# Reading a product in PSUM: two activations from the bank, scores copied by the maximum, a bank for helper products

## The chip, the cores and the metric

The kernel runs on one core of one Trainium2 chip. The metric is the device time of one execution in microseconds, median of several runs.

## The reference

Four batches of attention (8 heads, 576 tokens, 64 columns a head), and on its output, 2304 tokens by 512 columns, two expert layers one after the other. In the attention only scores within tau of their row's maximum count:

```python
scores = scale * np.matmul(q, k.transpose(0, 1, 3, 2))
thresh = np.max(scores, axis=-1, keepdims=True) - tau
scores = np.where(scores >= thresh, scores, -1000000000.0)
attn = np.exp(scores - np.max(scores, axis=-1, keepdims=True))
attn = attn / (np.sum(attn, axis=-1, keepdims=True) + 1e-09)
x = np.matmul(attn, v)
...
h = x @ w_in                                   # first layer, 512 -> 2048
P = a[0] + a[1] * h + a[2] * h**2 + a[3] * h**3
Q = 1.0 + np.abs(b[0]) * np.abs(h) + np.abs(b[1]) * h**2
y = (P / (Q + 1e-06)) @ w_out                  # 2048 -> 512
...
h = y @ w2_in                                  # second layer
g = np.where(h >= 1, h, np.where(h <= -1, 0.0, (h + 1) ** 2 / 4))
out = g @ w2_out
```

## The kernel before

Every number that enters a product is scaled and split into two float16 parts, high and low, and each product is three products of parts, added up in PSUM.

The work after the attention is cut into 192 steps: four batches, two layers, three blocks of 192 tokens, eight chunks of 256 hidden columns. A step is first_product (24 matmuls of 128x192 into one PSUM bank, tag "ph"; then the layer's function, rational or quadratic, on 128x384 elements; then split into gg on ACT and POOL) and, three steps later (LAG), second_product (24 matmuls into the accumulator, two banks, tag "acc").

rational begins with an ACT copy of the bank to h in SBUF, scaled (L517); all else reads h. ACT takes |h|, a logarithm and an exponential for the quotient, and one linear term; VectorE and POOL do the polynomials. For batch 0 the denominator's polynomial is done on POOL (L522, L523), for the others on VectorE (L520); s times h is POOL's for all (L527). quadratic too begins with an ACT copy (L581), then a Relu on ACT and two instructions on VectorE (L583, L584).

Attention of batch 0 runs first, beside the conversion of the first layer's weights. Attention of batch b + 1 is put beside the steps of batch b. It has 17 units per batch: five prepare inputs (units 0, 1, 2, 5 and 9), twelve do three rows each. A row is 128 queries of one head (att_rows): scores into two PSUM banks (tag "s", two tiles, for batch 0 a third in the accumulator's place), their maximum on VectorE (L406), a small instruction for the threshold (L407), the exponential on ACT (L368) and the mask on VectorE (L369), both from PSUM; then e is split into hl on ACT and POOL, transposed by DMA into eT, multiplied with v (tag "pv"; for batch 0 "ph"), divided by its sum (normalize), transposed by TensorE and stored as xT, from which the batch's first layer reads.

Small products that spread a maximum over the partitions (everywhere), the transposes in normalize and those of the output all take the bank with tag "pv". PSUM is full: one bank "pv", one "ph", two "acc", four "s".

A scheduler puts each engine's instructions in one order from priorities: a step's is its number, its second product's 1.5 later, a unit of attention's its due step less 1.5. The due steps are spread evenly over the window in ATTENTION, steps 6 to 46 for batch 1, 52 to 95 for batch 2, 100 to 143 for batch 3; the first layers of these batches begin at steps 48, 96 and 144. Each engine then works strictly in its order and waits where an input is late or a buffer is taken.

## Time and profile before

| | us |
|---|---|
| median of 3 runs | 1382.62 (1377.87 to 1388.38) |
| profiled execution | 1375.72 |
| its span, first to last instruction | 1373.6 |

Engines are PE (TensorE matmul), PEld (TensorE weight load), DVE (VectorE), ACT (ScalarE), POOL (GpSimd); SP issues the DMAs. Busy time is that in which an engine has an instruction at work; a VectorE or POOL instruction that is held up by the other counts as busy. A wait is named by the instruction whose end released it. L517 is line 517 of the kernel.

### The profile page before, as it was taken

To read this page: it belongs to the slowest core of one execution; us is meant where nothing else is said; L and a number is where in the kernel's file an instruction comes from. 1 tells how busy PE (TensorE), PEld (TensorE's weight loads), DVE (VectorE), ACT (ScalarE), POOL (GpSimd) and SP (SyncE) were. 2 spreads that over 40 slices of the span, in tenths; PEclk is the share of its full clock that TensorE was granted. 3 is DMA by queue.
4 is the path that set the end of the run, shared out by engine and by line. 5 is a ranking of instruction groups with operands and counts; after the bars stand their busy time and mean duration, and the time that the engine had idled before them with its cause. 6 is when DMAs were issued, how large, how long until landed. Compare 5 with 4: busy or idle time off the path is not lost. (4 is left out here: it accounts for less than half of the span.)

```text
span 1373.6 us, 31370 instructions
## 1 busy us (share of the span) xinstructions
PE 1075.8 (78%) x12498; PEld 979.7 (71%) x12498; DVE 1079.4 (79%) x2209; ACT 882.5 (64%) x1563; POOL 686.1 (50%) x716
## 2 busy tenths in 40 slices
PE   1545445566766398999978999987889898999998
PEld 1233234565655388898878889986788888988998
DVE  6787776899999967758999886599998665788422
ACT  4766555676756566667776666677766565777543
POOL 2755454887856454443655534435554344444221
PEclk9765556798887599999999999999999999999999
DMA  7879776325368745294238643923295449104200
GB/s 212 217 170 250 173 202 203 108 83 139 101 203 229 221 108 105 56 285 118 55 56 242 139 99 67 301 61 72 53 252 115 74 69 271 52 1 171 77 13 24
DMA packets 260274, 187.11 MB, mean 136 GB/s; under 512 B 220960, under 2 KB 233248, under 8 KB 251936
## 3 DMA queue, kind: packets, MB, share of 16 engines
q1 hardware_dynamic: 260128, 185.12, 52.0%
q8 instruction: 98, 1.61, 0.5%
q14 instruction: 48, 0.39, 0.1%
HBM read 106.96 MB, written 21.50 MB: 94 GB/s over the span
## 5 line engine op out<-in xcount | busy, mean ns | idle before, releaser
L651 PE MATMUL acc<-gg,wc 128*128 128x192 f16 x4608 | 447.8, 253 | 37.9 <-ACT gg L189 22.6
L651 PEld LDWEIGHTS <-wc 128*128 128x128 f16 x4608 | 401.4, 101 | 36.7 <-issue 33.3
L637 PEld LDWEIGHTS <-wc 128*128 128x128 f16 x4608 | 396.0, 100 | 38.4 <-issue 34.4
L190 POOL TENSOR_TENSOR gg<-t,gg 128x384 f16<-128x384 f32 x192 | 193.5, 1008 | 248.2 <-ACT gg L189 231.3
L637 PE MATMUL ph<-xT,wc 128*128 128x192 f16 x2304 | 225.2, 256 | 16.0 <-ACT t L517 14.4
L637 PE MATMUL ph<-yT,wc 128*128 128x192 f16 x2304 | 212.8, 247 | 10.6 <-ACT t L581 10.4
L189 ACT CAST gg<-t 128x384 f16<-128x384 f32 x192 | 97.5, 508 | 141.5 <-DVE t L531 64.2
L379 POOL TENSOR_TENSOR hl<-e,hl 128x512 f16<-128x512 f32 x144 | 181.7, 1261 | 0.0
L527 POOL TENSOR_TENSOR t<-t 128x384 f32<-128x384 f32 x96 | 117.1, 1221 | 120.1 <-ACT t L526 113.0
L377 ACT CAST hl<-e 128x576 f16<-128x576 f32 x144 | 96.0, 669 | 92.2 <-DMA eT<-hl 75.6
L368 ACT ACTIVATE e<-s,nt,con 128x576 f32<-128x576 f32 x144 | 117.9, 827 | 56.7 <-DVE nt L407 43.6
L378 POOL TENSOR_TENSOR hl<-e,hl 128x64 f16<-128x64 f32 x144 | 59.9, 416 | 183.5 <-ACT hl L377 159.8
L583 DVE SCALAR_TENSOR_TENSOR t<-t,c 128x384 f32<-128x384 f32 x96 | 68.3, 712 | 100.4 <-ACT t L582 98.7
L394 PE MATMUL pv<-v,eT 128*128 128x65 f16 (+1 forms) x2240 | 99.6, 208 | 45.5 <-DMA eT<-hl 16.8
L394 PEld LDWEIGHTS <-eT 128*128 128x128 f16 (+1 forms) x2240 | 93.4, 110 | 58.4 <-issue 38.4
L369 DVE SCALAR_TENSOR_TENSOR e<-s,nt,e 128x576 f32<-128x576 f32 x144 | 115.7, 807 | 23.8 <-ACT e L368 23.5
L357 PE MATMUL s<-qkT 128*128 128x512 f16 (+3 forms) x320 | 91.4, 327 | 50.1 <-DVE e L369 30.1
L406 DVE TENSOR_REDUCE mx<-s 128x1 f32<-128x576 f32 x144 | 106.3, 746 | 3.9 <-PE s L358 3.6
L528 DVE SCALAR_TENSOR_TENSOR t<-t,ka 128x384 f32<-128x384 f32 x96 | 87.7, 915 | 15.9 <-POOL t L527 15.9
L524 ACT ACTIVATE t<-t,lc 128x384 f32<-128x384 f32 x96 | 67.5, 703 | 38.2 <-DVE t L520 28.0
L530 DVE SCALAR_TENSOR_TENSOR t<-t,qc 128x384 f32<-128x384 f32 x96 | 78.6, 818 | 6.6 <-ACT t L525 6.6
L358 PE MATMUL s<-kT,qkT 128*128 128x512 f16 (+2 forms) x320 | 74.2, 325 | 9.9 <-DMA kT<-qkT 9.9
(170 smaller groups left out, 1708.8 us busy)
## 6 DMA issues: line engine op xcount, KB each, us to landing
wc<-scratch SPq DMA_DIRECT2D x56, 1024.0 KB, 6.1
rw<-in_moe_w_in_dram SPq DMA_DIRECT2D x16, 1024.0 KB, 5.7
rw<-in_moe_w_out_dram SPq DMA_DIRECT2D x16, 1024.0 KB, 5.6
scratch<-wc SPq DMA_DIRECT2D x8, 1024.0 KB, 4.6
scratch<-wh SPq DMA_DIRECT2D x16, 512.0 KB, 3.3
kT<-qkT SPq DMA_DIRECT2D x32, 144.0 KB, 2.5
rqk<-in_q_dram SPq DMA_DIRECT2D x16, 256.0 KB, 3.1
rqk<-in_k_dram SPq DMA_DIRECT2D x16, 256.0 KB, 3.0
```

What stands on the lines that cost most here:

```text
L189: A.copy(hi, src)
L190: G.tensor_tensor(lo, src, hi, op=ALU.subtract)
L357: T.matmul(s[rows, at : at + w], qkT[:, c, cols], k1[:, k0 : k0 + w], start=True, stop=False)
L368: A.activation(e, s, AF.Exp, bias=nb, scale=con[:, 0:1])
L369: V.scalar_tensor_tensor(e, s, th, e, op0=ALU.is_ge, op1=ALU.mult)
L377: A.copy(hi, e)
L379: G.tensor_tensor(lo_w, e[:, whole], hi[:, whole], op=ALU.subtract)
L394: T.matmul(pv[rows, 0:w], eT[:, c, cols], vv[:, h * NT + x if x < NT else H * NT + h, at : at + w], start=(n == 0), stop=(n == len(blocks) ...
L406: V.tensor_reduce(mx, s[:, 0:S], axis=AX.X, op=ALU.max)
L527: G.tensor_tensor(s, s, h, op=ALU.mult)
L637: last = T.matmul(ph[:, f, :], w[:, wx, kt, f * P : (f + 1) * P], rhs, start=(n == 0), stop=(n == 3 * KT - 1))
L651: T.matmul(dst, w[:, wx, f, d * P : (d + 1) * P], gg[:, gx, f, :], start=(i == 0 and f == 0 and n == 0 and d % 2 == 0), stop=(i == NCH - 1 ...
```

## The change

The bank of the first product is read more often and for longer: ACT's absolute value and linear term, and two VectorE instructions, take it from PSUM, with the scale moved into the constants (three small products per batch in moe1_consts, one per block in moe2_consts); the copy to h is gone in both functions. The denominator's polynomial and s times the product are VectorE's in all batches. There are two "ph" banks. In att_rows the maximum is found by an instruction that multiplies by 1, takes the larger of that and -3e38, writes the result to SBUF and accumulates the maximum; exponential and mask read that copy. One score tile is left, for batch 0 the accumulator's place is the second. Helper products, the transposes and the output's take a bank "aux"; "pv" is the weighted sum's alone. For batch 0 the weighted sum has both "ph" banks. Buffers: five shared temporaries in place of seven (a step of rational takes one in place of two) and three more of half the size ("poly"); two each of e and of the copy in place of three of e; one of xs in place of two. The windows of ATTENTION are 14 to 50, 60 to 100 and 108 to 147.

```diff
--- before.py
+++ after.py
@@ -26,10 +26,10 @@
 LAG = 3
 
 
-N_TEMP, N_WT, N_WH, N_GG, N_ROW = 7, 3, 2, 4, 3
-
-
-ATTENTION = {1: (6, 46), 2: (52, 95), 3: (100, 143)}
+N_TEMP, N_POLY, N_WT, N_WH, N_GG, N_ROW, N_SC = 5, 3, 3, 2, 4, 3, 2
+
+
+ATTENTION = {1: (14, 50), 2: (60, 100), 3: (108, 147)}
 WEIGHTS = (0, 20)
 
 
@@ -162,7 +162,7 @@
 
         r = small(n, name, keep)
         if place is None:
-            place = ps_1.tile([P, 512], F32, name="pm" + name, tag="pv")
+            place = ps_1.tile([P, 512], F32, name="pm" + name, tag="aux")
         pm = place[:, 0 : n * P].rearrange("p (n q) -> p n q", n=n)
         for i in range(n):
             T.matmul(pm[:, i], src[:, i : i + 1].to_broadcast([P, P]), ident, start=True, stop=True)
...
@@ -360,11 +360,10 @@
 
     def softmax(b, s, ab, con, nb, th, name):
 
-        s = s[:, 0:S]
         if b == 0:
             e = mp.tile([P, 2 * W], F32, name="e" + name, tag="tp", bufs=N_TEMP)[:, 0:S]
         else:
-            e = ap.tile([P, S], F32, name="e" + name, tag="e", bufs=N_ROW)
+            e = ap.tile([P, S], F32, name="e" + name, tag="e", bufs=N_SC)
         A.activation(e, s, AF.Exp, bias=nb, scale=con[:, 0:1])
         V.scalar_tensor_tensor(e, s, th, e, op0=ALU.is_ge, op1=ALU.mult)
         hl = ap.tile([P, 2 * S], F16, name="hl" + name, tag="hl", bufs=N_ROW)
@@ -399,15 +398,16 @@
         name = f"{b}_{pr}_{g}"
         rows = ROWS[3 * g : 3 * g + 3]
         for r, (t, ab) in enumerate(rows):
-            third = b == 0 and r == 2
-            s = ps_2.tile([P, 1024], F32, name=f"s{name}_{r}", tag="acc" if third else "s", bufs=1 if third else 2)
-            scores(s, t, ab, qkT, kT2)
+            other = b == 0 and r % 2 == 1
+            banks = ps_2.tile([P, 1024], F32, name=f"s{name}_{r}", tag="acc" if other else "s")
+            scores(banks, t, ab, qkT, kT2)
             mx, nt = small(1, f"mx{name}_{r}"), small(2, f"nt{name}_{r}")
-            V.tensor_reduce(mx, s[:, 0:S], axis=AX.X, op=ALU.max)
+            s = ap.tile([P, S], F32, name=f"sc{name}_{r}", tag="sc", bufs=N_SC)
+            V.tensor_scalar(s, banks[:, 0:S], 1.0, -LARGEST, op0=ALU.mult, op1=ALU.max, accum_out=mx)
             V.scalar_tensor_tensor(nt, con[:, 1:3], mx, con[:, 3:5], op0=ALU.mult, op1=ALU.add)
             eT = softmax(b, s, ab, con, nt[:, 1:2], nt[:, 0:1], f"{name}_{r}")
             if ab == 0:
-                pv = ps_1.tile([P, 512], F32, name=f"pv{b}_{pr}_{t}", tag="ph" if b == 0 else "pv")
+                pv = ps_1.tile([P, 512], F32, name=f"pv{b}_{pr}_{t}", tag="ph" if b == 0 else "pv", bufs=2 if b == 0 else 1)
                 pvs[t] = pv[:, 0 : 2 * (2 * D + 2)].rearrange("p (a d) -> p a d", a=2)
             if t < NT:
                 weighted(pvs[t][:, ab], slice(0, P), eT, slice(0, P), vv, h + ab, ab)
@@ -424,9 +424,9 @@
         rd = small(n, "rd" + name)
         V.tensor_scalar(rd, pv[:, 0:n, D], 1e-9 * E_SCALE, None, op0=ALU.add)
         V.reciprocal(rd, rd)
-        xs = ap.tile([P, 2, D], F32, name="xs" + name, tag="xs")
+        xs = ap.tile([P, 2, D], F32, name="xs" + name, tag="xs", bufs=1)
         V.tensor_tensor(xs, pv[:, 0:n, 0:D].to_broadcast([P, 2, D]), rd.unsqueeze(2).to_broadcast([P, 2, D]), op=ALU.mult)
-        pt = ps_1.tile([P, 512], F32, name="xt" + name, tag="pv")[:, 0:P]
+        pt = ps_1.tile([P, 512], F32, name="xt" + name, tag="aux")[:, 0:P]
         T.transpose(pt, xs.rearrange("p a d -> p (a d)"), ident)
         if t == NT:
             parts = [(slice(i * ST, (i + 1) * ST), i * ST, M, ST) for i in range(2)]
@@ -498,6 +498,8 @@
         ka = sp.tile([P, NCH, 4], F32, name=f"ka{b}", tag="ka", bufs=2)
         V.tensor_tensor(ka, k8.unsqueeze(2).to_broadcast([P, NCH, 4]), pc.unsqueeze(1).to_broadcast([P, NCH, 4]),
                         op=ALU.mult)
+        for n in range(1, 4):
+            V.tensor_tensor(ka[:, :, n:], ka[:, :, n:], sc.unsqueeze(2).to_broadcast([P, NCH, 4 - n]), op=ALU.mult)
 
         iy = sp.tile([P, 1], F32, name=f"iy{b}", tag="iy", bufs=3)
         V.tensor_scalar(iy, f, f_max[0][1], 2.0, op0=ALU.mult, op1=ALU.mult)
@@ -508,24 +510,21 @@
         t = mp.tile([P, 2, W], F32, name=name, tag="tp", bufs=N_TEMP)
         return t[:, 0], t[:, 1]
 
-    def rational(ph, i, consts, name, on_vector):
+    def rational(ph, i, consts, name):
+
 
 
         sc, ka = consts[0], consts[1][:, i, :]
-        src = ph.rearrange("p f t -> p (f t)")
-        (h, s), (u, r) = temp("t0" + name), temp("t1" + name)
-        A.activation(h, src, AF.Copy, scale=sc[:, i : i + 1])
-        A.activation(u, h, AF.Abs)
-        if on_vector:
-            V.scalar_tensor_tensor(u, u, qc[:, 0:1], u, op0=ALU.add, op1=ALU.mult)
-        else:
-            G.tensor_scalar(r, u, 1.0, qc[:, 0:1], op0=ALU.mult, op1=ALU.add)
-            G.tensor_tensor(u, r, u, op=ALU.mult)
+        p = ph.rearrange("p f t -> p (f t)")
+        u, r = temp("t0" + name)
+        s = mp.tile([P, W], F32, name="t1" + name, tag="poly", bufs=N_POLY)
+        A.activation(u, p, AF.Abs, scale=sc[:, i : i + 1])
+        A.activation(s, p, AF.Identity, bias=ka[:, 2:3], scale=ka[:, 3:4])
+        V.scalar_tensor_tensor(u, u, qc[:, 0:1], u, op0=ALU.add, op1=ALU.mult)
+        V.tensor_tensor(s, s, p, op=ALU.mult)
+        V.scalar_tensor_tensor(s, s, ka[:, 1:2], p, op0=ALU.add, op1=ALU.mult)
         A.activation(r, u, AF.Ln, bias=lc[:, 1:2], scale=lc[:, 0:1])
         A.activation(r, r, AF.Exp, bias=lc[:, 2:3], scale=-1.0)
-        A.activation(s, h, AF.Identity, bias=ka[:, 2:3], scale=ka[:, 3:4])
-        G.tensor_tensor(s, s, h, op=ALU.mult)
-        V.scalar_tensor_tensor(s, s, ka[:, 1:2], h, op0=ALU.add, op1=ALU.mult)
         V.scalar_tensor_tensor(s, s, ka[:, 0:1], r, op0=ALU.add, op1=ALU.mult)
         V.scalar_tensor_tensor(u, u, qc[:, 1:2], r, op0=ALU.add, op1=ALU.mult)
         V.scalar_tensor_tensor(u, u, 2.0, s, op0=ALU.subtract, op1=ALU.mult)
@@ -567,6 +566,7 @@
         V.tensor_scalar(su, sri, fr, 2.0**27, op0=ALU.mult, op1=ALU.mult)
         V.tensor_scalar(iv, iv, rk, 2.0**-56, op0=ALU.mult, op1=ALU.mult)
         V.tensor_scalar(sg, w2b, iv, rk, op0=ALU.mult, op1=ALU.mult)
+        V.tensor_tensor(su, su, sg, op=ALU.mult)
         io = c[:, 4 * NCH :]
         V.tensor_scalar(io, fr, fr, 2.0**56, op0=ALU.mult, op1=ALU.mult)
         V.tensor_scalar(io, io, f_max[1][1], None, op0=ALU.mult)
@@ -576,13 +576,12 @@
 
 
         top, bias, su, sg, _ = (x[:, i : i + 1] if e < 4 else x for e, x in enumerate(consts))
-        src = ph.rearrange("p f t -> p (f t)")
-        h, u = temp("t2" + name)
-        A.activation(h, src, AF.Copy, scale=sg)
-        A.activation(u, h, AF.Relu, bias=bias, scale=su)
+        p = ph.rearrange("p f t -> p (f t)")
+        u, g = temp("t2" + name)
+        A.activation(u, p, AF.Relu, bias=bias, scale=su)
         V.scalar_tensor_tensor(u, u, top, u, op0=ALU.min, op1=ALU.mult)
-        V.tensor_tensor(u, h, u, op=ALU.max)
-        return u
+        V.scalar_tensor_tensor(g, p, sg, u, op0=ALU.mult, op1=ALU.max)
+        return g
 
     yT, y_scale = {}, {}
 
...
@@ -622,10 +621,10 @@
 
     chunks = {}
 
-    def first_product(m, b, j, i, consts, on_vector):
+    def first_product(m, b, j, i, consts):
         name = f"{m}_{b}_{j}_{i}"
         w = chunks[m, i][:, 0:HALF].rearrange("p (x kt f) -> p x kt f", x=2, kt=KT)
-        ph = ps_1.tile([P, 512], F32, name="ph" + name, tag="ph")[:, 0:W].rearrange("p (f t) -> p f t", f=NF)
+        ph = ps_1.tile([P, 512], F32, name="ph" + name, tag="ph", bufs=2)[:, 0:W].rearrange("p (f t) -> p f t", f=NF)
         for f in range(NF):
             n = 0
             for kt in range(KT):
@@ -636,7 +635,7 @@
                         rhs = yT[b, j][:, xx * KT + kt, :]
                     last = T.matmul(ph[:, f, :], w[:, wx, kt, f * P : (f + 1) * P], rhs, start=(n == 0), stop=(n == 3 * KT - 1))
                     n += 1
-        g = rational(ph, i, consts, name, on_vector) if m == 0 else quadratic(ph, i, consts, name)
+        g = rational(ph, i, consts, name) if m == 0 else quadratic(ph, i, consts, name)
         gg = mp.tile([P, 2, NF, TB], F16, name="gg" + name, tag="gg", bufs=N_GG)
         hi, lo = (gg[:, x].rearrange("p f t -> p (f t)") for x in range(2))
         split(hi, lo, g)
...
```

## Rows read from the trace of the kernel before

**Rows 1.** Windows: stretch, length, busy PE, PEld, DVE, ACT, POOL; clock, DMA share, GB/s.

```profile
0.00:228.00 228.00, 103.23 (x877) 69.14 (x877) 169.27 (x382) 131.42 (x213) 109.15 (x126) 0.65 0.79 206
228.00:470.00 242.00, 150.32 (x1394) 132.40 (x1394) 231.55 (x378) 155.67 (x259) 172.11 (x140) 0.80 0.50 153
470.00:600.00 130.00, 116.70 (x1563) 109.86 (x1564) 90.49 (x225) 77.68 (x146) 59.87 (x79) 0.96 0.56 123
600.00:768.00 168.00, 148.13 (x1734) 138.85 (x1732) 158.11 (x324) 124.45 (x230) 85.90 (x88) 0.94 0.57 148
768.00:895.00 127.00, 122.54 (x1659) 115.68 (x1657) 88.22 (x204) 83.75 (x156) 57.50 (x75) 1.00 0.59 139
895.00:1058.00 163.00, 140.60 (x1659) 130.41 (x1657) 156.86 (x328) 118.79 (x219) 85.26 (x89) 0.97 0.47 112
1058.00:1170.00 112.00, 103.01 (x1378) 95.79 (x1375) 68.32 (x155) 67.86 (x125) 46.95 (x58) 1.00 0.63 138
1170.00:1270.00 100.00, 93.36 (x1086) 90.84 (x1084) 85.02 (x152) 74.13 (x139) 46.92 (x42) 0.97 0.19 68
1270.00:1374.00 104.00, 97.85 (x1169) 96.77 (x1166) 31.60 (x66) 48.73 (x83) 22.39 (x25) 0.98 0.12 40
```

**Rows 2.** Single lines on VectorE: count, then ns min/median/max, first and last start.

```profile
L406 DVE TENSOR_REDUCE mx<-s x144: 730/745/758, 35.0 to 1131.4; 128x1 f32<-128x576 f32 x144
...
L369 DVE SCALAR_TENSOR_TENSOR e<-s,nt,e x144: 790/806/819, 42.2 to 1137.6; 128x576 f32<-128x576 f32 x144
...
L528 DVE SCALAR_TENSOR_TENSOR t<-t,ka x96: 600/618/2479, 245.9 to 1265.1; 128x384 f32<-128x384 f32 x96
```

**Rows 3.** VectorE groups from 228 to 470 us: busy us, mean ns, idle before.

```profile
L528 DVE SCALAR_TENSOR_TENSOR t<-t,ka 128x384 f32<-128x384 f32 x24 | 27.7, 1156 | 1.8 <-POOL t L527 1.8
...
L530 DVE SCALAR_TENSOR_TENSOR t<-t,qc 128x384 f32<-128x384 f32 x24 | 26.5, 1103 | 0.6 <-ACT t L525 0.6
...
L529 DVE SCALAR_TENSOR_TENSOR t<-t,ka,t 128x384 f32<-128x384 f32 x24 | 24.3, 1012 | 0.5 <-ACT t L525 0.5
...
L531 DVE SCALAR_TENSOR_TENSOR t<-t,t 128x384 f32<-128x384 f32 x24 | 21.1, 881 | 0.0
...
L407 DVE SCALAR_TENSOR_TENSOR nt<-con,mx 128x2 f32<-128x2 f32 x17 | 10.0, 588 | 0.0
```

**Rows 4.** VectorE groups from 600 to 768 us.

```profile
L528 DVE SCALAR_TENSOR_TENSOR t<-t,ka 128x384 f32<-128x384 f32 x24 | 19.8, 824 | 3.6 <-POOL t L527 3.6
...
L520 DVE SCALAR_TENSOR_TENSOR t<-t,qc 128x384 f32<-128x384 f32 x24 | 16.6, 691 | 2.2 <-ACT t L518 2.1
```

**Rows 5.** Groups of the whole span, ACT.

```profile
L517 ACT ACTIVATE t<-ph,sc 128x384 f32<-128x384 f32 x96 | 54.9, 572 | 31.9 <-PE ph L637 23.1 <-POOL gg L190 5.2 <-PE pv L394 1.8
```

**Rows 6.** Groups of the whole span, POOL.

```profile
L527 POOL TENSOR_TENSOR t<-t 128x384 f32<-128x384 f32 x96 | 117.1, 1221 | 120.1 <-ACT t L526 113.0 <-DMA rqk<-in_q_dram 3.3 <-ACT g L559 3.3
...
L523 POOL TENSOR_TENSOR t<-t 128x384 f32<-128x384 f32 x24 | 30.3, 1263 | 0.8
...
L522 POOL TENSOR_SCALAR t<-t,qc 128x384 f32<-128x384 f32 x24 | 23.7, 989 | 20.3 <-ACT t L518 20.3
```

**Rows 7.** A single line on ACT: ns min/median/max.

```profile
L313 ACT ACTIVATION_READ_ACCUMULATOR qk<-rqk x8: 185/187/198, 10.5 to 121.1; 128x1 f32 x8
```

**Rows 8.** TensorE groups from 470 to 600 us.

```profile
L394 PE MATMUL pv<-v,eT 128*128 128x65 f16 (+3 forms) x392 | 15.1, 197 | 2.6 <-DVE xT L439 2.3 <-DMA eT<-hl 0.3
L357 PE MATMUL s<-qkT 128*128 128x512 f16 (+3 forms) x44 | 10.6, 289 | 4.6 <-DVE e L369 2.8 <-DVE rd L425 1.8
L358 PE MATMUL s<-kT,qkT 128*128 128x512 f16 (+3 forms) x44 | 8.5, 286 | 0.0
```

**Rows 9.** Waits of the whole span: us in total, times, longest.

```profile
PE s L357 <- DVE e L369: 30.1, 28, 4.0
```

**Rows 10.** Timeline, VectorE and ACT around 1150 us: start, us.

```profile
1149.76 0.23 DVE L439 TENSOR_TENSOR xT<-xt,xT 128x64 f16<-128x64 f32 x1 [0.28 <-ACT xT L438]
...
1150.89 0.58 ACT L517 ACTIVATE t<-ph,sc 128x384 f32<-128x384 f32 x1 [1.16 <-PE ph L637]
```

More of the change, by code (lines that the diff above doesn't have):

```diff
@@ L227, in convert @@
         if m == 0 and x == 0:
-            pg = ps_1.tile([P, 512], F32, name="pg" + name, tag="pv")[:, 0:CF]
+            pg = ps_1.tile([P, 512], F32, name="pg" + name, tag="aux")[:, 0:CF]
             cols = hi.rearrange("p (kt f) -> p kt f", kt=KT)
@@ L610, in end_moe2 @@
             n, t, p0 = c1 - c0, c0 // P, c0 % P
-            pt = ps_1.tile([P, DM], F32, name=f"pt{b}_{j}_{c0}", tag="pv")
+            pt = ps_1.tile([P, DM], F32, name=f"pt{b}_{j}_{c0}", tag="aux")
             for d in range(KT):
@@ L706, in tile_attention_moe_moe2 @@
                     consts[m, b, j] = moe2_consts(b, j)
-            gg, last = first_product(m, b, j, i, consts[m, b, j], b > 0)
+            gg, last = first_product(m, b, j, i, consts[m, b, j])
         pending.append((n, m, b, j, i, gg, last))
```

## The prediction

> **What bounds the kernel now.** I read the windows view first, cut where one layer of one batch ends and the next begins. The reader should compare the busy time of each engine with the length of the stretch [rows 1]. In the three stretches in which the first expert layer of a batch runs beside the next batch's attention (228 to 470, 600 to 768, 895 to 1058 us), VectorE is busy for 231.55 of 242, 158.11 of 168 and 156.86 of 163 us: VectorE sets their length. In the three that follow (second expert layer, 470 to 600, 768 to 895, 1058 to 1170) VectorE has a third free, and TensorE is busy for 116.70 of 130, 122.54 of 127 and 103.01 of 112 us: TensorE sets those. In the first 228 us no engine is full; DMA is busiest (0.79). From 1170 to 1270 no attention is left and VectorE and TensorE both have a little room; the last stretch is TensorE's. So work that leaves VectorE in the first layers pays, work that arrives on TensorE in the second layers costs, and ACT and POOL are full nowhere.
>
> Second, I read what VectorE's instructions last. The mask (L369), which reads the scores from PSUM and e from SBUF, takes 790 to 819 ns, always; the maximum (L406) 730 to 758, always; but L528, with both tensors in SBUF, spreads from 600 to 2479 [rows 2]. In the stretch where POOL is busy for 172 of 242 us, L528 to L531 average 1156, 1012, 1103 and 881 ns [rows 3]; in 600 to 768, with POOL at 86 of 168, L528 takes 824 and L520 691 [rows 4]. A VectorE instruction with two SBUF tensors pays for what POOL does at the time; one that reads PSUM doesn't. Over 600 ns the price is 0.44 us at POOL's 71%, and about 0.15 at 51%.
>
> **The change part by part.**
>
> *Activations read PSUM.* Per step one ACT copy of 572 ns (L517, and L581 likewise) goes [rows 5], 192 times, 110 us of ACT. ACT is off the path in every stretch, so by itself this is worth nothing. Abs, Identity and Relu now read PSUM instead of SBUF; I take their durations as they are.
>
> *The polynomial leaves POOL.* L527 (1220 ns, 96 times) and, for batch 0, L522 and L523 (989 and 1263 ns, 24 times each) go [rows 6]: 83 us of POOL between 228 and 470, 29 us in each later first layer. POOL falls there from 71% to some 40%, and from 51% to some 35%. VectorE gets one product more (s times the PSUM product), and L528 reads PSUM now. For a 384-column instruction that reads PSUM I bound the price by L369 scaled to the columns (806 x 384/576 = 0.54 us) and by L528's shortest, 0.60; I take 0.60, for both. The four others keep two SBUF tensors: 0.60 plus contention, which I take as 0.12 in batch 0's layer (between nothing and today's 0.44) and 0.10 later.
> Batch 0: today 1.16 + 1.01 + 1.10 + 0.88 = 4.15 us of VectorE a step. After: four at 0.72 (with the product in Abs, which POOL did) and two at 0.60, 4.08. Over 24 steps -2 us.
> Later: today 0.82 + 0.74 + 0.73 + 0.72 + 0.69, whose two ends are in [rows 4], some 3.7 us; after, 4 x 0.70 + 1.20 = 4.0. Over 24 steps +7 us.
> Second layer: L584 reads PSUM instead of SBUF; I count no change, between -0.2 and 0 us a step. The few instructions on constants come once a batch or block and are left out.
>
> *Scores.* L406 becomes an instruction that also writes 576 columns to SBUF and then gives its accumulator. The trace has no such one on VectorE. Below, nothing extra; above, what ACT's own accumulator read costs, 187 ns [rows 7]; I take 0.09. The mask then has two SBUF tensors: +0.10 to +0.44, I take 0.14. So +0.23 us a row, 36 rows a batch, some 9 of them left in each of the three stretches that VectorE bounds. In the first 228 us that is 8 us of VectorE (19 at the upper ends), covered by its 59 idle us; I count 2.
> A rule speaks against this part: the Trainium skill (SBUF — State Buffer, "Who interferes with whom") says that a VectorE instruction with two SBUF inputs and a GpSimd one that reads SBUF shut each other out, the later waiting for the whole of the earlier. Today's mask, with one SBUF input, is flat, and L528, with two, is not [rows 2]: the trace agrees. By that rule at its dearest (0.44 us on 27 masks) the sum below would be 1367; by the flat row of the mask (nothing) it would be 1355.
>
> *The order.* ATTENTION moves. A batch has 17 units of work, five of them preparation, and unit n is due at first + n x (last - first)/17 steps, less 1.5. Before step 24 of each batch's two layers 15 of the 36 rows were due (units 3, 4, 6, 7, 8); with the new windows 6 (units 3, 4), for all three batches. So 9 rows go from the first layer into the second. A row costs VectorE at least 0.75 + 0.59 + 0.81 = 2.15 us [rows 2, 3], so 19 us leave each VectorE-bound stretch. They cost TensorE 15.1 us for 28 rows and 10.6 + 8.5 for 22 [rows 8], 1.4 us a row, so 13 us arrive in each stretch that TensorE bounds.
>
> *Banks.* The product has two PSUM banks, helper products their own. One score tile instead of two is left beside the accumulator, held for the copy instead of up to the mask. Today TensorE loses 30 us before scores to the mask [rows 9]; the copy comes some microseconds earlier than the mask, but there is one tile for it, so I leave this wait as it is. Behind a waiting score matmul stand the products of both layers in TensorE's queue, and behind those ACT and VectorE. A product's bank is now held until VectorE's second reading instead of ACT's copy, which two banks cover as long as that comes within one step.
>
> **The sum**, against the profiled execution (1375.7 us, span 1373.6; 7 us under the median of the runs shown).
> First 228 us: +2.
> VectorE-bound: -19 - 2 + 2 (rows that stay) = -19 of VectorE between 228 and 470, -19 + 7 + 2 = -10 in each of the other two: -39, at today's filling of 94 to 96% about -41.
> TensorE-bound: +13 each, against the TensorE idle of 13, 4.5 and 9 us [rows 1], of which I let the new banks fill half: +7, +11, +9 = +27.
> 1170 to 1270: the step loses POOL's hop (1.22 us) and an ACT copy from its chain while VectorE has 15 us left: -5 (0 to -10).
> Last stretch: 0.
> +2 - 41 + 27 - 5 = -17. 1375.7 - 17 = **1359 us**.
>
> **Rivals.**
>
> *Attention comes too late (slower).* The last unit that the next batch's first token block needs is unit 15. Its due step goes from 41.3 to 45.8, 89.9 to 95.3, 137.9 to 142.4, and that block's layer starts at 48, 96, 144. The trace speaks for it: in batch 3 the last needed piece of xT is written at 1149.76 and the layer's first activation reads at 1150.89 [rows 10]; there is no slack to give. The delay is 4.5 to 5.4 steps of about 5.4 us (130 us for 24 steps), 24 to 29 us a batch. Against it: with VectorE freer in the second layer the way from scores to xT can shorten, and VectorE works on meanwhile. If half is lost at all three starts, +39 on the sum: some 1398; if all, 1437. It decides from about 7 us a batch on. The single score tile and two e buffers in place of three, which make TensorE and ACT wait in order, would add to the same delay.
>
> *TensorE takes it all (no change).* If the banks fill none of TensorE's idle time, the three +13 stand whole, the first-layer gain is only the moved rows' and the end gains nothing: +2 - 41 + 39 = 0, 1376. For it: TensorE is at 90 to 96% there.
>
> *The engines are freed more than priced (much faster).* If the second bank, the helpers' bank and POOL's lighter load fill TensorE's idle 26 us and cover the new rows, and contention nearly goes (4 x 0.6 + 1.2 = 3.6 a step, 10 us a batch): -41 - 30 + 2, with -10 at the end, some 1300 to 1320. For it: the 0.44 us an instruction of [rows 3], POOL's load falling by half.
>
> *Contention goes to the mask instead.* At 0.44 us on each of the some 27 masks left in VectorE-bound stretches the cost is 8 us more than counted: inside the forecast's range, so without a chance of its own.
>
> **Numbers.** Forecast (1332 to 1369) 0.42, at 1359; no change (1370 to 1390) 0.22; slower (at 1398, from 1390 up) 0.20; much faster (at 1315, under 1332) 0.16. About 1% is what a measurement can tell from no change, 1368.8 to 1396.4 on the shown median. Faster by more than 1%: 0.42 less 0.03 of its upper edge, plus 0.16, 0.55. Within 1%: 0.22 + 0.03 and a fifth of the slower case, 0.29. Slower: the rest of it, 0.16. The range 1308 to 1400 leaves out about 0.09 of the slower case's 0.20 and 0.05 of the fast one's 0.16; the forecast's own is 1332 to 1369.
>
> **What would show it.** VectorE's first-layer stretches shorter by some 10 to 20 us each and the second-layer ones longer by about 10. L527's successor flat near 0.56 to 0.60 us, the mask spread like L528 today, L406's successor near 0.75 plus a small accumulator row. POOL busy some 170 us less in all, ACT some 110. It is wrong if TensorE idles at 48, 96, 144 steps waiting for xT, if TensorE's waits for the score copy exceed the 30 us it lost to L369, or if the three TensorE-bound stretches grow by more than 13 us each.

## The result, and the profile after

The changed kernel takes 1336.53 us (median of 4 runs, 1335.04 to 1340.14) against 1380.24 (the three runs of the table above and one more, 1375.78 to 1388.38): a ratio of 0.9681, with an interval of 0.9628 to 0.9733. Forecast were 1359 and a range of 1308 to 1400: the direction and the range hold, the size does not. The profiled execution is the longest of its four (1340.14, span 1338.3), that of before (1375.72) lies at the short end of its four, so the two traces differ by 35 us where the medians differ by 44.

The engines' busy time on the page of the changed kernel (share of the span, instructions):

```profile
PE 1055.2 (79%) x12498; PEld 962.3 (72%) x12498; DVE 1078.3 (81%) x2497; ACT 796.2 (59%) x1371; POOL 514.2 (38%) x572
```

POOL does 172 us less (foreseen: some 170) and ACT 86 less (110). VectorE has 288 instructions more and works as long as before, in a shorter span.

Windows of the changed kernel, cut at each layer's first activation (columns as in [rows 1]):

```profile
0.00:231.00 231.00, 102.82 (x877) 69.97 (x878) 180.37 (x416) 130.73 (x209) 113.77 (x125) 0.63 0.78 203
231.00:451.00 220.00, 136.69 (x1358) 121.96 (x1358) 206.04 (x443) 141.11 (x231) 84.21 (x63) 0.81 0.54 169
451.00:585.00 134.00, 123.85 (x1620) 113.08 (x1620) 99.39 (x258) 76.39 (x135) 61.71 (x82) 0.96 0.60 121
585.00:713.00 128.00, 115.79 (x1347) 111.13 (x1345) 117.04 (x265) 86.26 (x154) 34.14 (x38) 0.95 0.47 132
713.00:858.00 145.00, 131.07 (x1754) 120.37 (x1752) 116.24 (x290) 81.87 (x146) 69.01 (x88) 1.00 0.69 140
858.00:983.00 125.00, 110.26 (x1331) 104.49 (x1331) 117.45 (x270) 88.70 (x159) 34.75 (x40) 0.99 0.46 119
983.00:1130.00 147.00, 134.70 (x1793) 123.13 (x1793) 117.05 (x297) 81.85 (x147) 71.23 (x87) 1.00 0.62 136
1130.00:1228.50 98.50, 95.78 (x1183) 94.80 (x1182) 88.89 (x195) 72.50 (x136) 22.50 (x25) 1.00 0.29 84
```

[Rows 1] are cut at round times, so the table below cuts both traces at the first activation of each layer and counts the rows of attention (L406) in each stretch. "First 0" is the first expert layer of batch 0.

| stretch | before, us (rows) | after, us (rows) | difference | forecast |
|---|---|---|---|---|
| opening | 227.7 | 231.0 | +3.3 | +2 |
| first 0 | 248.4 (17) | 219.6 (9) | -28.8 | -20 |
| second 0 | 124.6 (19) | 134.6 (27) | +10.0 | +7 |
| first 1 | 144.2 (14) | 127.8 (7) | -16.4 | -10.5 |
| second 1 | 129.0 (22) | 144.5 (28) | +15.5 | +11 |
| first 2 | 136.4 (12) | 125.4 (9) | -11.0 | -10.5 |
| second 2 | 140.5 (24) | 147.2 (28) | +6.7 | +9 |
| first 3 | 115.6 | 98.2 | -17.4 | -5 |
| second 3 | 107.1 | 109.8 | +2.7 | 0 |
| sum | 1373.6 | 1338.3 | -35.3 | -17 |

The pattern is the one foreseen: VectorE's stretches shrink, TensorE's grow. The first layers lose 28 us more than forecast, first 3, where no attention is left, 12 of them; the other stretches give 9 back. A part of first 3's loss is the cut alone: 96 matmuls fewer fall into it than before (1183, 1279 before), and the last stretch is 2.7 longer; the two together give 14.7 us where 5 were foreseen.

VectorE's single lines in the changed kernel (count, ns min/median/max, as in [rows 2]):

```profile
L368 DVE SCALAR_TENSOR_TENSOR e<-sc,nt,e x144: 792/817/2599, 42.2 to 1130.3; 128x576 f32<-128x576 f32 x144
...
L406 DVE TENSOR_SCALAR_CACHE_REDUCE sc<-s x144: 727/746/759, 37.9 to 1127.4; 128x576 f32<-128x576 f32 x144
L406 DVE DVE_READ_ACCUMULATOR sc<-s x144: 73/80/85, 38.6 to 1128.1; 128x1 f32 x144
...
L524 DVE TENSOR_TENSOR t<-t,ph x96: 528/542/555, 247.9 to 1226.4; 128x384 f32<-128x384 f32 x96
L525 DVE SCALAR_TENSOR_TENSOR t<-t,ka,ph x96: 586/604/616, 248.9 to 1227.0; 128x384 f32<-128x384 f32 x96
L523 DVE SCALAR_TENSOR_TENSOR t<-t,qc x96: 592/612/2167, 231.6 to 1225.8; 128x384 f32<-128x384 f32 x96
```

The two that read the product in PSUM (L524, L525) are flat, the mask (L368), flat before, now has the long tail that L528 had. Its group over the whole span (busy us, mean ns, idle before):

```profile
L368 DVE SCALAR_TENSOR_TENSOR e<-sc,nt,e 128x576 f32<-128x576 f32 x144 | 134.7, 936 | 41.0 <-ACT e L367 40.6
```

### The profile page after: what moved, and what is told of

It is laid out like the page before. It is cut to its first block, busy times and chain, and to the rows that moved or that the text cites. A ratio compares the mean times of both kernels' runs of the same rounds, so it can differ in the third digit from the quotient of the medians.

```text
span 1338.3 us, 31403 instructions
## 1 busy us (share of the span) xinstructions
PE 1055.2 (79%) x12498; PEld 962.3 (72%) x12498; DVE 1078.3 (81%) x2497; ACT 796.2 (59%) x1371; POOL 514.2 (38%) x572
## 4 chain that ended last, share of the span: by engine, by line
PE 31%; DVE 28%; DMA 13%; issue 11%; POOL 7%; ACT 6%; SPq 2%; ACTq 0%; DVEq 0%; POOLq 0%
PE acc L650 14%; PE ph L636 13%; DMA eT<-hl 8%; POOL hl L378 4%; DVE e L368 4%; DMA qkT<-qk 3%; DVE sc L406 3%; PE pv L393 2%; DVE wt L207 2%; DVE t L530 2%; DVE t L529 2%; DVE t L523 2%; DVE nt L407 1%; DVE t L528 1%; DVE wt L208 1%
## 5 line engine op out<-in xcount | busy, mean ns | idle before, releaser
L650 PE MATMUL acc<-gg,wc 128*128 128x192 f16 x4608 | 426.2, 247 | 11.4 <-POOL gg L190 6.1
L636 PEld LDWEIGHTS <-wc 128*128 128x128 f16 x4608 | 392.9, 100 | 43.8 <-DVE t L525 24.7
L650 PEld LDWEIGHTS <-wc 128*128 128x128 f16 x4608 | 384.5, 98 | 13.4 <-issue 11.5
L636 PE MATMUL ph<-yT,wc 128*128 128x192 f16 x2304 | 219.2, 247 | 2.5 <-DVE t L583 1.9
L367 ACT ACTIVATE e<-sc,nt,con 128x576 f32<-128x576 f32 x144 | 124.0, 865 | 74.5 <-DVE nt L407 62.6
L368 DVE SCALAR_TENSOR_TENSOR e<-sc,nt,e 128x576 f32<-128x576 f32 x144 | 134.7, 936 | 41.0 <-ACT e L367 40.6
L393 PE MATMUL pv<-v,eT 128*128 128x65 f16 (+1 forms) x2240 | 107.0, 207 | 73.8 <-DMA eT<-hl 58.7
L406 DVE TENSOR_SCALAR_CACHE_REDUCE sc<-s 128x576 f32<-128x576 f32 x144 | 107.5, 747 | 14.1 <-PE s L358 13.2
L521 ACT ACTIVATE t<-ph,sc 128x384 f32<-128x384 f32 x96 | 55.3, 576 | 64.1 <-PE ph L636 63.9
L581 ACT ACTIVATE t<-ph,c 128x384 f32<-128x384 f32 x96 | 63.9, 667 | 47.1 <-PE ph L636 45.3
L358 PEld LDWEIGHTS <-qkT 128*128 128x128 f16 (+1 forms) x320 | 32.3, 111 | 73.3 <-issue 54.5
```

The costliest lines, as they stand in the source:

```text
L358: T.matmul(s[rows, at : at + w], qkT[:, c, cols], k2[:, k0 : k0 + w], start=False, stop=True)
L367: A.activation(e, s, AF.Exp, bias=nb, scale=con[:, 0:1])
L368: V.scalar_tensor_tensor(e, s, th, e, op0=ALU.is_ge, op1=ALU.mult)
L393: T.matmul(pv[rows, 0:w], eT[:, c, cols], vv[:, h * NT + x if x < NT else H * NT + h, at : at + w], start=(n == 0), stop=(n == len(blocks) ...
L406: V.tensor_scalar(s, banks[:, 0:S], 1.0, -LARGEST, op0=ALU.mult, op1=ALU.max, accum_out=mx)
L636: last = T.matmul(ph[:, f, :], w[:, wx, kt, f * P : (f + 1) * P], rhs, start=(n == 0), stop=(n == 3 * KT - 1))
```

## The experiments

All were timed in three rounds beside the kernel before. Behind each median stands its ratio to the kernel before, with an interval of 95%. The kernel before took 1377.4 to 1380.9 us beside the different experiments, so a difference between two of them is good to some 3 us. Rows are counted as in the table above. In the names, "functions" are `rational` and `quadratic`, "helpers" the small products that got a bank of their own.

**1. The windows alone, and the change without them.** Kernel before with the new ATTENTION; changed kernel with the old:

```diff
-ATTENTION = {1: (6, 46), 2: (52, 95), 3: (100, 143)}
+ATTENTION = {1: (14, 50), 2: (60, 100), 3: (108, 147)}
```

> The kernel before with the new windows alone (14 to 50, 60 to 100, 108 to 147). Theory A: between 1370 and 1400, since moved rows give VectorE's stretches some 35 us and cost TensorE's some 30, and the first layers may start late. Theory B: 1340 to 1355. Theory C: 1375 to 1385.

> The changed kernel with the old windows of the attention (6 to 46, 52 to 95, 100 to 143), all else as changed. Changed kernel 1336.5 us, before 1380.2. If the gain is the functions' (theory A: POOL's hop and the contention leave the first layers), the old windows cost some 5 to 15 us: 1342 to 1352. If it is the order's (theory B: rows moved out of VectorE's stretches), most of the gain goes: 1365 or more. If it is the second product bank's (theory C), nothing changes: within 4 us of 1336.

Measured: the windows alone 1402.5 us, 1.0149 (1.0127 to 1.0171), slower than before; the change without them 1360.03, 0.9848 (0.9833 to 0.9863). The first lies just above the range of theory A, the second between those of A and B. So the windows are worth -24 us inside the change and +22 outside it. On the old kernel they do take rows from the first layers (17, 14 and 12 rows become 11, 9 and 9; those stretches lose 13, 5 and 2 us), but the second layers grow by 28, 19 and 3. One of these, batch 0's, in the windows view:

```profile
465.90:618.40 152.50, 132.25 (x1664) 121.36 (x1662) 99.92 (x235) 88.57 (x161) 62.58 (x86) 0.90 0.61 131
```

TensorE has 132 us of work in 152, and a granted clock of 0.90. Of its waits there (us in total, times, longest; 20 us in all) half are the first of these:

```profile
PE pv L394 <- DVE xT L439: 10.5, 5, 2.9
...
PE ph L637 <- ACT xT L438: 0.3, 1, 0.3
```

The first line is the accumulation of the next rows, waiting until a helper has left the bank that both use. The second is xT itself, late at the end of the stretch: the last 15 matmuls of batch 1's first step start at 615.7 us, when ACT has written the piece of xT that they read, straight behind the transpose that it comes from. So do the same 15 of batches 2 and 3, at 902.6 and 1180.9. This is the slower rival's mechanism, attention that comes too late, but in the old kernel with new windows.

**2. The helpers' own bank.** Changed kernel, the tag of the helpers' tiles back to the one of the attention's accumulation, at four places:

```diff
-        pt = ps_1.tile([P, 512], F32, name="xt" + name, tag="aux")[:, 0:P]
+        pt = ps_1.tile([P, 512], F32, name="xt" + name, tag="pv")[:, 0:P]
```

> The changed kernel with helper products and transposes back in the weighted sum's bank (one bank of PSUM left unused). By the prediction's step on the banks, some 0 to 10 us slower: 1336 to 1346. If the own bank is what makes the new windows bearable, 1355 or more.

Measured: 1381.09 us, 1.0006 (0.9992 to 1.0021): without this one bank the whole gain is gone. The first layers keep theirs (215.2, 123.7 and 124.0 us); the second layers take 151.7, 158.4 and 166.1 in place of 134.6, 144.5 and 147.2. Windows of this kernel, two of these three:

```profile
445.80:597.50 151.70, 130.55 (x1647) 118.45 (x1648) 108.72 (x264) 76.91 (x138) 67.03 (x86) 0.91 0.62 130
...
1003.60:1169.80 166.20, 141.59 (x1754) 127.02 (x1754) 118.81 (x295) 81.71 (x148) 73.45 (x89) 0.93 0.55 124
```

TensorE stands idle 21 and 25 us, against 10 and 12 in the changed kernel's second 0 and second 2, and its granted clock is 0.91 and 0.93, not 0.96 and 1.00. What it waits for in the one between (721.2 to 879.6 us):

```profile
PE xt L430 <- DVE xs L428: 7.4, 5, 2.6
...
PE pv L393 <- DVE xT L439: 6.0, 5, 2.2
...
PE s L357 <- DVE sc L406: 5.0, 5, 2.9
```

The first two are the bank going from an accumulation to a transpose and back (the transpose waits for its input too, which it needs in either kernel). With banks of their own, the changed kernel's waits in the same stretch (713 to 858 us) are on a DMA, and on the copy for 0.3 us (of what the fence leaves out, none is over 0.8):

```profile
PE pv L393 <- DMA eT<-hl: 11.9, 11, 2.6
...
PE s L357 <- DVE sc L406: 0.3, 1, 0.3
```

Waiting is not the whole loss. With 83 rows in both kernels the three second layers together lose 50 us: 30 are idle time of TensorE, and in 20 it is busy for longer with the same work (409 us after 390), while its granted clock is lower.

**3. The score copy.** Changed kernel, scores read in PSUM again:

```diff
-            s = ap.tile([P, S], F32, name=f"sc{name}_{r}", tag="sc", bufs=N_SC)
-            V.tensor_scalar(s, banks[:, 0:S], 1.0, -LARGEST, op0=ALU.mult, op1=ALU.max, accum_out=mx)
+            s = banks[:, 0:S]
+            V.tensor_reduce(mx, s, axis=AX.X, op=ALU.max)
```

> The changed kernel with the score copy alone undone: the maximum by a reduction, exponential and mask read the one score tile in PSUM, which is so held up to the mask. The mask is flat again near 0.81 us instead of 0.94 (144 x 0.13 = 19 us of VectorE less). If the copy's early release of the tile matters, TensorE waits longer before scores and the time is 1350 or more; if the copy is only a price, 1325 to 1336.

Measured: 1390.93 us, 1.0102 (1.0068 to 1.0136). The mask is flat again (787 to 819 ns). Second layers of 157.4, 174.4 and 162.3 us. Over the whole span TensorE's wait before scores is on the mask,

```profile
PE s L357 <- DVE e L368: 70.8, 41, 5.7
```

where the changed kernel waits less, and on the copy:

```profile
PE s L357 <- DVE sc L406: 47.0, 27, 4.6
...
PE ph L636 <- DVE t L525: 31.7, 15, 7.5
```

Most of both totals lies outside the second layers: the opening alone has 29.4 us of the first and 31.5 of the second. In the three second layers the wait is 23.7 us with the scores in PSUM and 5.2 with the copy. Together these layers lose 68 us, with five rows more: 36 in idle time of TensorE and 32 in longer busy time, at granted clocks of 0.88, 0.88 and 0.92. The copy's price (0.08 us a row and a dearer mask) buys the one score tile's early release.

**4. The product's second bank.** Changed kernel, the product's tag with one bank (batch 0's accumulations, under the same tag, have one too):

```diff
-        ph = ps_1.tile([P, 512], F32, name="ph" + name, tag="ph", bufs=2)[:, 0:W]
+        ph = ps_1.tile([P, 512], F32, name="ph" + name, tag="ph", bufs=1)[:, 0:W]
```

> The changed kernel with one bank for the product (and for batch 0's weighted sum) in place of two. Theories A and B: up to 10 us slower than 1336, since a bank is held until VectorE's second reading. Theory C: 1360 or more, and the first layer of batch 3, which has no attention beside it, returns from 98 to about 115 us.

Measured: 1478.82 us, 1.0706 (1.0678 to 1.0735): dearer by far than theories A and B expected, and in the range of theory C, the second bank (whose other conditions fail: windows_old is not within 4 us of 1336, copy_kept not between 1336 and 1345). The last first layer, with no attention in it, takes 121.9 us in place of 98.2: here a bank that is held until VectorE's second reading must be doubled. A part of the 142 us is another order: in this kernel 21 rows fall into each of the other three first layers, in the changed kernel 9, 7 and 9. The wait of the last fence's second line grows to

```profile
PE ph L636 <- DVE t L525: 77.3, 57, 5.5
```

**5. Copy and polynomials, taken apart.** copy_kept is the changed kernel with the old functions (copies on ACT, polynomials on POOL; six temporary buffers). copy_kept_no_pool is the same with the polynomials on VectorE, in SBUF:

```diff
-        if on_vector:
-            V.scalar_tensor_tensor(u, u, qc[:, 0:1], u, op0=ALU.add, op1=ALU.mult)
-        else:
-            G.tensor_scalar(r, u, 1.0, qc[:, 0:1], op0=ALU.mult, op1=ALU.add)
-            G.tensor_tensor(u, r, u, op=ALU.mult)
+        V.scalar_tensor_tensor(u, u, qc[:, 0:1], u, op0=ALU.add, op1=ALU.mult)
...
-        G.tensor_tensor(s, s, h, op=ALU.mult)
+        V.tensor_tensor(s, s, h, op=ALU.mult)
```

> The changed kernel with both functions as they were: ACT copies the product to SBUF, s times h and batch 0's polynomial on POOL; two product banks, score copy, bank for helpers and windows as changed (six shared temporaries, since seven don't fit). Theory A: most of the gain goes, 1365 to 1385, and the first layer of batch 3 takes about 115 us again. Theories B and C: 1336 to 1345, and about 98 us.

> The kernel with the copy kept (1378.7 us), its polynomials moved from POOL to VectorE: ACT still copies the product to SBUF and all VectorE instructions read SBUF. If it is POOL that the gain comes from (its hop in the chain and its load on VectorE's instructions), most of it is here: 1338 to 1350, and the first layer of batch 3 takes about 98 to 102 us instead of 111. If it is the copy's end (ACT's time, a shorter chain, PSUM operands free of contention), it stays above 1362 and at about 108 us.

Measured: 1378.7 us, 0.9981 (0.9969 to 0.9994), and 1350.53, 0.9785 (0.9764 to 0.9807). Of the 42 us that the functions are worth in the changed kernel, 28 come with work that goes from POOL to VectorE, the engine that was full, and 14 with the copies' end, which also lets two VectorE instructions read PSUM (`rational` takes 108.1 us of VectorE in batch 0's first layer with the copy, 99.7 in the changed kernel, 144 instructions in both). (The second lies at the upper edge of what was expected if POOL is the cause.) Windows of batch 0's first layer and of the last first layer of copy_kept_no_pool:

```profile
231.00:463.50 232.50, 143.61 (x1395) 125.75 (x1395) 215.48 (x442) 152.55 (x256) 83.77 (x63) 0.77 0.53 160
...
1137.40:1239.90 102.50, 100.64 (x1244) 99.83 (x1243) 98.31 (x193) 86.69 (x161) 26.83 (x26) 1.00 0.30 94
```

and of copy_kept:

```profile
231.60:474.00 242.40, 148.44 (x1389) 131.07 (x1389) 221.68 (x389) 152.94 (x257) 177.07 (x135) 0.79 0.51 151
...
1158.20:1269.20 111.00, 103.54 (x1238) 101.82 (x1236) 92.35 (x169) 85.99 (x161) 54.88 (x50) 0.97 0.27 85
```

In the last first layer VectorE has 24 instructions more and is busy only 6 us longer, and the stretch is 8 us shorter. In batch 0's, with 11 rows in both, it has 53 instructions more and is busy for 6 us less.

**6. Is it contention?** Two kernels load POOL again behind each first-layer split, without touching the chain of the function: pool_loaded with subtractions that read and write SBUF, pool_memset with three times as many memsets, which only write. Both write into a buffer that is done with, and change no result.

```diff
+        for _ in range(0 if m else 3 if b == 0 else 1):
+            G.tensor_tensor(r, r, r, op=ALU.subtract)
```

```diff
+        for _ in range(0 if m else 9 if b == 0 else 3):
+            G.memset(r, 0.0)
```

> The changed kernel with POOL loaded again: behind each first-layer split POOL multiplies nothing of use, one 128x384 instruction on SBUF per step (three for batch 0), whose result nobody reads. If VectorE's contention with POOL is the cause, batch 0's first layer goes from 220 to 235 us or more and the whole to 1352 to 1365. If it is the hop in the chain, at most 6 us are lost: 1336 to 1343.

> The changed kernel with POOL busy as in the loaded one (1388.7 us), but with instructions that read nothing: three memsets of 128x384 in the place of each multiplication. If POOL's load cost VectorE its reading side (contention), most of the 52 us do not come: 1336 to 1350, and VectorE is busy some 206 us in batch 0's first layer instead of 230. If the load only delays the splits in POOL's queue, it is 1370 or more.

Measured: 1388.71 us, 1.0066 (1.0041 to 1.009), and 1344.92, 0.9756 (0.972 to 0.9793). The load of pool_loaded, as a single line:

```profile
L643 POOL TENSOR_TENSOR t<-t x144: 817/1133/1805, 252.7 to 1278.5; 128x384 f32<-128x384 f32 x144
```

and that of pool_memset, three to each of the former:

```profile
L643 POOL MEMSET t<- x432: 410/418/959, 252.6 to 1229.5; 128x384 f32 x144
```

Batch 0's first layer, windows of pool_loaded

```profile
231.60:479.00 247.40, 149.82 (x1369) 132.11 (x1368) 230.42 (x439) 141.28 (x229) 168.79 (x135) 0.75 0.47 147
```

and of pool_memset:

```profile
231.50:458.40 226.90, 145.90 (x1399) 127.94 (x1399) 207.09 (x453) 142.83 (x232) 162.01 (x281) 0.78 0.53 166
```

POOL is busy for 169 and 162 us, nearly as long as in the kernel before (176 from first activation to first activation), but VectorE needs 230 us with the one and 207 with the other, the changed kernel's own 206. In the last first layer L523, the instruction that the load slows most, takes 1055 ns in pool_loaded,

```profile
L523 DVE SCALAR_TENSOR_TENSOR t<-t,qc 128x384 f32<-128x384 f32 x24 | 25.3, 1055 | 0.7 <-ACT t L521 0.6
```

642 in the changed kernel and 638 in pool_memset,

```profile
L523 DVE SCALAR_TENSOR_TENSOR t<-t,qc 128x384 f32<-128x384 f32 x24 | 15.3, 638 | 0.7 <-ACT t L521 0.7
```

and that layer lasts 108.3 (with one row of attention), 98.2 and 98.9 us. The two kernels lie 44 us apart and differ in whether POOL's load reads. So it is what POOL reads that VectorE pays for, not that POOL is busy and not its place in the chain. By the rule of the Trainium skill that the prediction weighs (SBUF — State Buffer, "Who interferes with whom"), a VectorE instruction with two SBUF inputs contends with a GpSimd one that reads SBUF, not with one that only writes it. These runs agree (1055 and 638 ns). The 52 us that pool_loaded loses are more than the 16 to 28 expected, and more than the 42 that the functions are worth; these runs do not show why.

**7. Scores and banks without the rest.** copy_kept with the old windows:

> The kernel with the copy kept (1378.7 us) and the old windows: of the change only the score copy and the banks. The new windows alone cost the kernel before 22 us, and gained 23 on the changed one. If score copy and banks are what turns this, the old windows cost here, 1385 to 1400; if it is the functions, this is faster than 1378.7: 1355 to 1372.

Measured: 1403.83 us, 1.017 (1.0148 to 1.0191), dearer still than the 1385 to 1400 expected. The score copy and the banks alone cost 23 us, the windows alone 22, and both together (copy_kept) are 2 us faster than before.

**8. Later windows.** Changed kernel, ATTENTION moved on:

```diff
-ATTENTION = {1: (14, 50), 2: (60, 100), 3: (108, 147)}
+ATTENTION = {1: (18, 50), 2: (64, 100), 3: (112, 147)}
```

and, in windows_latest_2, {1: (18, 50), 2: (68, 99), 3: (116, 147)}.

> The changed kernel with windows that begin four steps later still and end as they do (18 to 50, 64 to 100, 112 to 147). From the old windows to the new the time fell by 23 us. If VectorE's first-layer stretches still bound it, three rows more leave each of them, 1328 to 1336; if TensorE's stretches or the late start take it, 1340 to 1360.

> Windows 18 to 50, 68 to 99, 116 to 147: the later start (1325.5 us) four steps later again for batches 2 and 3, so that none of their rows is due in a first layer (6 and 7 are there now). In batch 0 nine rows fewer shortened the first layer by 29 us and lengthened the second by 19. If the same rate holds, 1312 to 1320; if attention now ends too late or TensorE has no room left for six more rows, 1325 to 1345.

Measured: 1325.47 us (1324.21 to 1327.08), 0.9619 (0.9594 to 0.9645), and 1323.73 (1323.41 to 1324.53), 0.9597 (0.958 to 0.9615): faster than both kernels. All 36 rows leave batch 0's first layer; windows of the first of the two:

```profile
230.30:420.60 190.30, 120.80 (x1223) 112.41 (x1222) 172.03 (x351) 122.22 (x202) 69.71 (x42) 0.84 0.46 161
420.60:574.20 153.60, 138.07 (x1770) 122.29 (x1771) 135.35 (x345) 92.26 (x163) 76.53 (x101) 0.97 0.74 156
```

First 0 gives 29 us more, second 0 takes 19. In the later batches 6 and 7 rows stay in the first layers with both windows: the due steps order the work but do not hold it back, and the last windows brought some 2 or 3 us and not the 5 to 13 expected.

## Why the prediction was right in direction and wrong in size

**What held.** VectorE sets the first layers and TensorE the second; the table's signs are all as forecast but for the last stretch, forecast at 0. The instructions that read PSUM take 0.54 and 0.60 us (0.60 taken), the accumulator's read 0.080 (0.09), the mask 936 - 806 = 0.13 us more (0.14).

**What held by luck.** TensorE's three stretches grow by 32 us in all, forecast 27. But that sum let the new banks fill half of TensorE's idle time under 27 rows more. Only 18 rows came, and the idle time was not filled: it grew from 26 to 36 us. Windows of the kernel before, cut as in the table, to set beside those of the changed kernel above:

```profile
476.10:600.70 124.60, 115.46 (x1542) 108.79 (x1542) 85.02 (x197) 76.98 (x145) 56.05 (x76) 0.98 0.54 119
...
744.90:873.90 129.00, 121.85 (x1635) 113.56 (x1635) 96.09 (x226) 83.36 (x153) 59.05 (x78) 1.00 0.60 135
...
1010.30:1150.90 140.60, 130.56 (x1698) 119.62 (x1697) 100.33 (x241) 85.35 (x159) 62.03 (x76) 0.99 0.61 130
```

Fewer rows and more idle time nearly cancel. The helpers' bank kept that idle time from growing further (to 67 us, experiment 2), but nothing of what there was before was filled.

**Rows moved: fewer than counted.** 8, 7 and 3 rows left the first layers, not 9 each, and 17, 14 and 12 had been there, not 15: a due step is a priority, and an idle engine takes rows earlier. That alone would have taken some 9 x 2.15 = 19 us of VectorE from the gain, and spared TensorE's stretches some 9 x 1.4 = 13. Two small numbers beside this are off, and little hangs on them: for the copy's price the prediction lets 9 rows stay in each first layer where its own count leaves 6 (9, 7 and 9 stayed), and both upper ends of that price make 23 us for the opening, not 19.

**The step that failed: contention in the later first layers, the "+7".** Of the 28 us that the first layers lose beyond the forecast, 12 lie in first 3, 9 in first 0 and 6 in first 1. Experiment 6 shows what was at stake: 44 us between a POOL that reads and one that only writes. The term was forecast at +7 us of VectorE for each of first 1 and first 2; it came out at -0.6 and about 0. The prediction took four instructions of 0.60 + 0.10 and two of 0.60, 4.0 us a step, against 3.7 before. VectorE groups of the changed kernel between 585 and 713 us (first 1; busy us, mean ns, idle before):

```profile
L523 DVE SCALAR_TENSOR_TENSOR t<-t,qc 128x384 f32<-128x384 f32 x24 | 17.3, 719 | 3.4 <-ACT t L521 3.4
L529 DVE SCALAR_TENSOR_TENSOR t<-t,qc 128x384 f32<-128x384 f32 x23 | 14.9, 649 | 0.0
L528 DVE SCALAR_TENSOR_TENSOR t<-t,ka,t 128x384 f32<-128x384 f32 x23 | 14.5, 629 | 3.9 <-ACT t L527 3.9
L525 DVE SCALAR_TENSOR_TENSOR t<-t,ka,ph 128x384 f32<-128x384 f32 x23 | 14.0, 607 | 0.3
L524 DVE TENSOR_TENSOR t<-t,ph 128x384 f32<-128x384 f32 x24 | 13.1, 544 | 0.0
L530 DVE SCALAR_TENSOR_TENSOR t<-t,t 128x384 f32<-128x384 f32 x22 | 12.1, 551 | 0.3
```

The six sum to 3.70 us, and the four with two SBUF tensors average 0.64. Here POOL is busy for 34 of 128 us, a share of 27%; the prediction reckoned with some 35% and with a price nearly in step with it. So the extra instruction cost nothing: VectorE's time in `rational` over that stretch is 85.8 us after 86.4, and 87.0 after 87.0 in first 2 (sums of its durations by line in the two traces). Together with what the rows' absence spared, first 1 lost 16.4 us, not 10.5, and first 2 lost 11.0 with three rows gone in place of nine.

**The same step at the end: "-5 (0 to -10)".** The prediction saw VectorE with 15 us left there [rows 1] and priced only the shorter chain. But the instructions on the chain were slowed by POOL too. In first 3 of the changed kernel

```profile
L523 DVE SCALAR_TENSOR_TENSOR t<-t,qc 128x384 f32<-128x384 f32 x24 | 15.4, 642 | 0.7 <-ACT t L521 0.6
...
L528 DVE SCALAR_TENSOR_TENSOR t<-t,ka,t 128x384 f32<-128x384 f32 x24 | 14.7, 613 | 5.9 <-ACT t L527 5.9
```

answer to these of the kernel before, between 1150.9 and 1266.5 us:

```profile
L528 DVE SCALAR_TENSOR_TENSOR t<-t,ka 128x384 f32<-128x384 f32 x24 | 21.5, 894 | 5.9 <-POOL t L527 5.9
L520 DVE SCALAR_TENSOR_TENSOR t<-t,qc 128x384 f32<-128x384 f32 x24 | 21.2, 882 | 5.3 <-ACT t L518 5.3
```

In experiment 6 the last two stretches take 217.5 us in pool_loaded (one row of attention among them) and 208.7 in pool_memset: up to 8.8 us are POOL's reading. In experiment 5 they take 218.8 and 209.7, where POOL's reading and its hop in the chain end together. Both are more than the 5 us forecast for the hop and the copy.

**Batch 0's first layer: the functions as forecast, the rest not looked at.** VectorE groups of the changed kernel between 231 and 451 us:

```profile
L523 DVE SCALAR_TENSOR_TENSOR t<-t,qc 128x384 f32<-128x384 f32 x24 | 20.7, 863 | 3.4 <-ACT t L521 3.4
L528 DVE SCALAR_TENSOR_TENSOR t<-t,ka,t 128x384 f32<-128x384 f32 x24 | 18.7, 778 | 1.9 <-ACT t L527 1.7
L530 DVE SCALAR_TENSOR_TENSOR t<-t,t 128x384 f32<-128x384 f32 x24 | 16.8, 702 | 0.0
L529 DVE SCALAR_TENSOR_TENSOR t<-t,qc 128x384 f32<-128x384 f32 x24 | 16.0, 672 | 0.0
```

The four average 0.75 us (0.72 taken; 0.88 to 1.16 in [rows 3]), so six instructions take what four took, as forecast, and fewer rows left than counted. But the prediction looked only at the functions and the rows. Summed by function, VectorE's time there falls by 28 us: 14 in the rows' reductions and masks, 5 in the weights' bit operations (55.3 to 50.6 us for the same 42 instructions, beside a quieter POOL), and the rest spread over smaller ones, of the preparation above all. 19 us had been forecast for VectorE.

**The rival "engines freed more than priced"** named half of this, at 1300 to 1320 and a chance of 0.16: contention nearly went (3.70 us a step where it says 3.6), but TensorE's idle time, which it says is filled, grew. The time came out at the lower edge of the forecast's own range (1332 to 1369). "Attention comes too late" did not happen: the last piece of xT that the first block needs is written 8.6, 4.6 and 7.1 us before the first activation reads. In the kernel before it was 1.4 us for batch 3, not the 0.9 of [rows 10]: the second piece of that tile, which the prediction took, belongs to the next block. TensorE did wait 0.3 us for the first, so that there was no slack holds. "TensorE takes it all" is what the change becomes without the helpers' bank (1381).

**A sign that misled.** The prediction said it would be wrong if waits for the score copy passed the 30 us of [rows 9]. They are 47.0 us and the kernel is faster; so large a total over the span says little where it does not lie in a stretch that TensorE sets (31.5 us of it are in the opening, 5.2 in the three second layers). Another sign, TensorE's stretches growing by more than 13 us, came for one of three (second 1, 15.5).

**What a sum of parts could not give.** Taken out of the change one at a time, the parts cost 23.5 (windows), 42 (functions), 44.5 (helpers' bank), 54 (score copy) and 142 us (second product bank, with another order), 306 together for a change that gains 44; put in alone, the windows cost 22 us and the scores with the banks 23. The parts hold each other up: later rows need a TensorE that does not wait in order for shared banks.

**Open.** Why POOL's load costs more in pool_loaded than its end brought is not shown. Each edit makes the scheduler order the instructions anew (rows per stretch differ between the kernels), so a single difference holds a share of order that these runs do not separate. How much of pool_memset's 8 us over the changed kernel is order (12 rows in first 0, not 9) isn't settled either.

## What to carry to other kernels

When work leaves GpSimd, price what VectorE's other two-operand SBUF instructions get back, in every stretch, before the work that arrives; an edit that adds VectorE instructions can shorten VectorE's busy time (53 more and 6 us less in experiment 5). When rows are moved into a stretch that TensorE sets, look first for tiles in PSUM that two uses pass to and fro, for a priority alone made this kernel slower (by 22 us), and the same priority with separate banks and the score copy made it faster (by 25, scores_and_banks against copy_kept). And try a schedule's constants again after the change: four steps later was worth another 11 us.

## What had not been expected of the hardware

GpSimd memsets that kept POOL about as busy as before (51 us of first 3's 99) left VectorE's instructions as short as without them (638 against 642 ns). An instruction that writes 576 columns of the scores to SBUF and finds their maximum takes as long as the reduction alone (746 and 745 ns), and VectorE's accumulator read costs 80 ns, less than half of ACT's 187 [rows 7]. The price of contention is not in step with POOL's share: for the instructions above over 0.60 us it is some 0.44 at 71%, 0.15 at 51% [rows 4] and again at 38% (batch 0 after), 0.04 at 27%.
